# Mix products between two column groups of an attention product, and tiles turned by TensorE in an attention, channel-mix and expert kernel

## The chip, the cores and the metric

The kernel runs on one core of a Trainium2 chip. The metric is the device time of one execution in microseconds (us). Before the change the median of three runs is 1425.25 us (1423.19, 1425.25 and 1433.6).

## The reference, cut to what matters

```python
def reference(q, k, v, p, w_ch1, w_ch2, w_gate, w_local, w1, w2):
    # attention: B=8, H=8, S=576, D=64, 32 packed queries p per head
    packed = softmax(p @ k.T / 8) @ v            # 32 x 64 per head
    x = softmax(q @ packed.T / 8) @ packed       # (8, 576, 512) once the heads are side by side
    # mix: two-dimensional Fourier transform, layer norm, channel MLP 512 -> 2048 -> 512
    u = x + real(fft(fft(x, axis=1), axis=2))
    x = u + relu(layernorm(u) @ w_ch1) @ w_ch2
    # experts: 8 of them, 512 -> 1024 -> 512, one per token
    logits, gate = x @ w_gate, sigmoid(x @ w_local)
    for each token s of a batch in turn:
        e = argmax(logits[s]) if s == 0 or gate[s] < 0.5 else e of token s - 1
        out[s] = softmax(logits[s])[e] * (relu(x[s] @ w1[e]) @ w2[e])
    return out
```

## The kernel before

**Numbers and tiles.** Every fp32 operand is held as a high and a low fp16 half, and a product is three matmuls (`PASS`: high by high, high by low, low by high). Tokens go in tiles of 128; a block of the main part is one batch's 512 tokens, and the 64 tokens that each batch has over are gathered in two half blocks, "R0" and "R1".

**Main part.** The loop runs over the blocks 0, 1, 2, R0, 3, 4, 5, 6, R1, 7. For each, `Mix.mm1` (L1129, PSUM tiles hp) and `Mix.mm2` (L1149, PSUM tiles acc) make the channel MLP, 512 columns a matmul. After each few matmuls `tick` advances generators in the background, each at its own rate: the attention of the next block (with its Fourier transform), `after_mix` of the block before, and, from block 1 on, the cast of the expert weights into halves (`ew`). What a generator issues at a tick stands at that place of the queue of its engine, so the yields of a generator set where its work lies between the mix matmuls. A scheduler puts the instructions of each engine into their final order before the kernel runs, close to that order.

**The attention's cosine product.** Late in the attention, `products(cs, hf, tiles)` (L574 for the first two row tiles, L571 for the third) multiplies the even and odd parts eh with a table of cosines cst into the PSUM tile bp. For cs = 0 there are two column groups, hf = 0 and 1, with one bp tile each. `halves` (L579 on ScalarE, L580 on VectorE) copies a finished bp tile to SBUF. The bp tiles, the logits' lp, and others come from `att`, a PSUM pool with two buffers: a tile that is asked for waits until the last reader of the tile two before it is done.

**After the mix.** `after_mix` takes the tiles of a finished block one by one. VectorE makes a scale for each row, ScalarE (L1180) and VectorE (L1181) write the two halves into xh (tag hl, three buffers, which the gathered xg tiles use too), SyncE's queue (SP) transposes xh with a DMA into xt (L1188, one buffer) and writes xh to the DRAM table XS (L1189). A few yields later `logits` multiplies xt with the gate's weights (L1166, L1168, 18 and 9 columns, PSUM tile lp), and VectorE reduces lp to lsum (L1170). For block 7, whose mix ends the main part, `after_mix` runs at the start of the expert phase, beside the first expert blocks.

**Expert phase.** A line of 34 blocks of 128 tokens with one expert and 3 shared blocks with two experts of 64 tokens each. `load_x` gathers the tokens (L1491, GpSimd) and transposes them with a DMA on SP (L1495). `e1` (L1536, PSUM ehp, 96 matmuls of 128 columns) and `e2` (L1597, PSUM eo, 24 matmuls of 512 columns) are the two layers, and `e1` of a block runs ahead of `e2` of the block before. Expert weights come from DRAM by `weights` (L1517, queue SP) in quarters of 512 KB, into three slots. A shared block's first layer, `e1_two` (L1559), leaves its halves hh with tokens on partitions; `turned` (L1577) turns them by 16 matmuls against an identity into an `att` tile, from which ScalarE (L1582) and VectorE (L1580) copy them to hx. Before, `turned` is handed to `e2` of the block in front and runs between its matmuls. A second generator, `r1`, holds the rest of `after_mix` and the second routing, and must be done before the sixth block from the start.

Of the kernel before, what the change touches and what calls it, by code (L numbers as in the profile page):

```python
# [192 lines left out]
def _build(tc, nc, ctx, A, stop):  # L193
# [150 lines left out]
    def attention(b):  # L344
# [79 lines left out]
        for hf in range(2):  # L424
# [9 lines left out]
            n = 0  # L434
# [147 lines left out]

        for hf in range(2):
            products(0, hf, (0, 1))
        yield
        for hf in range(2):
            products(0, hf, (2,))
# [569 lines left out]
                        nc.vector.tensor_tensor(ut, ut, self.acc[j], op=ALU.add)  # L1157
            tick(0.25)

    def after_mix(tiles):  # L1160
        xt = None

        def logits(col):
            lp = att(f"lp{col}")
            for c in range(4):
                nc.tensor.matmul(lp[:, :18], xt[:, c], wgh[:, c].rearrange("p y e -> p (y e)"), start=c == 0, stop=False,  # L1166
                                 skip_group_check=True)
                nc.tensor.matmul(lp[:, :9], xt[:, 4 + c], wgh[:, c, 0], start=False, stop=c == 3, skip_group_check=True)  # L1168
            lsum = wp.tile([128, 9], F32, tag="lsum", name=f"lsum{col}", bufs=2)
            nc.vector.tensor_reduce(lsum, lp[:, :18].rearrange("p (y e) -> p e y", y=2), axis=AX.X, op=ALU.add)  # L1170
            nc.vector.tensor_scalar(LG[:, col], lsum, RSC[:, col:col + 1], 2.0 ** -20, ALU.mult, ALU.mult)

        for j, (ut, col) in enumerate(tiles):
            sc = wp.tile([128, 2], F32, tag="rsc", name=f"rsc{col}", bufs=2)
            nc.vector.tensor_reduce(sc[:, 0:1], ut, axis=AX.X, op=ALU.max, apply_absolute_value=True)
            nc.vector.tensor_scalar(RSC[:, col:col + 1], sc[:, 0:1], 1e-30, 0.25, ALU.max, ALU.mult)
            nc.vector.reciprocal(sc[:, 1:2], RSC[:, col:col + 1])
            yield
            hl = wp.tile([128, 1024], F16, tag="hl", name=f"xh{col}", bufs=3)
            nc.scalar.activation(hl[:, :512], ut, AF.Copy, scale=sc[:, 1:2])  # L1180
            nc.vector.scalar_tensor_tensor(hl[:, 512:], ut, sc[:, 1:2], hl[:, :512], ALU.mult, ALU.subtract)  # L1181
            yield
            if j:
                yield
                logits(tiles[j - 1][1])
                yield
            xt = wp.tile([128, 8, 128], F16, tag="xt", name=f"xt{col}", bufs=1)
            nc.sync.dma_start_transpose(out=xt, in_=hl)  # L1188
            nc.sync.dma_start(XS[128 * col:128 * col + 128], hl)  # L1189
            yield  # L1190
        for _ in range(4):
            yield
        logits(tiles[-1][1])
        yield
# [288 lines left out]

    w1b, w2b = [], []
    xg, xt, regs, hb = {}, {}, {}, {}

    def load_x(b):
        mp = M["p"]
# [33 lines left out]
    def load_w2(b, k0=0, k1=4):  # L1522
        weights(b, w2b, WS2, k0, k1)

    def e1(b, todo=()):

        ht = M["q"].tile([128, 2, 2, 512], F16, tag="hx", name=f"hx{b}", bufs=3)
        r = place_of(b)
        for fg in range(2):
            hp = (psM, psO)[fg].tile([128, 512], F32, tag="ho"[fg], name=f"ehp{b}_{fg}")  # L1530
            for f in range(4):
                n = 0
                cols = slice(128 * f, 128 * f + 128)
                for c in range(4):
                    for (x, y) in PASS:
                        nc.tensor.matmul(hp[:, cols], w1b[r][:, 2 * c + fg, x, cols], xt[b][:, 4 * y + c],  # L1536
                                         start=n == 0, stop=n == 11, skip_group_check=True)
                        n += 1
                if f % 2 == 0:
                    for fn, t in todo:  # L1540
                        fn(t, 2 * fg + f // 2, 2 * fg + f // 2 + 1)
                if f < 3:
                    tick()
            nc.scalar.activation(ht[:, fg, 0], hp, AF.Relu)  # L1544
# [1 line left out]
            tick()  # L1546
        hb[b] = ht

    def e1_two(b, todo=()):

        hh = M["q"].tile([128, 2, 2, 512], F16, tag="hx", name=f"hh{b}", bufs=3)
        for fg in range(2):
# [16 lines left out]
    def turned(b):  # L1569
        hh = hb[b]  # L1570
        ht = M["q"].tile([128, 2, 2, 512], F16, tag="hx", name=f"hx{b}", bufs=3)
        for fg in range(2):
            for x in range(2):
                tp = att(f"ht{b}_{fg}_{x}")
                for f in range(4):
                    cols = slice(128 * f, 128 * f + 128)
                    nc.tensor.matmul(tp[:, cols], hh[:, fg, x, cols], idh, start=f == 0, stop=True,  # L1577
                                     skip_group_check=True)
                if x:
                    nc.vector.tensor_copy(ht[:, fg, x], tp)  # L1580
                else:
                    nc.scalar.copy(ht[:, fg, x], tp)  # L1582
                yield
        hb[b] = ht

    def e2(b, todo=(), beside=None):
        h = hb.pop(b)
        op = psO.tile([128, 512], F32, tag="o", name=f"eo{b}")
        two = b >= FIRST
# [2 lines left out]
        for f in range(8):  # L1592
# [7 lines left out]
            if f % 2 == 0:  # L1600
                for fn, t in todo:
                    fn(t, f // 2, f // 2 + 1)
            if beside is not None and 2 <= f:
                next(beside, None)
            tick()
        ys = wp.tile([128, 512], F32, tag="U", name=f"ys{b}", bufs=8)
        nc.scalar.activation(ys, op, AF.Copy, scale=scl[:, b:b + 1])  # L1607
# [46 lines left out]
        prev = mix  # L1654
    for f in range(16 - LEAD, 16):
        prev.mm2(f)
    last = after_mix(prev.tiles)
    drain(r0)
    wctx.close()
    M["q"] = ctx.enter_context(tc.tile_pool(name="mq", bufs=1, side="right"))  # L1660
# [33 lines left out]

    def open_one(i):
        b = line[i]
        (e1_two if b >= FIRST else e1)(b, todo("e1", i))

    open_one(0)
    for i, b in enumerate(line):  # L1700
        if i + RB == NEARLY:
            drain(r1)
        if i + AHEAD < len(line):
            load_x(line[i + AHEAD])
        beside = None
        if i + 1 < len(line):
            open_one(i + 1)
            if line[i + 1] >= FIRST:
                beside = turned(line[i + 1])
        if i == len(line) - 1:  # L1710
            left = nc.values_load(used[0:1, 2:3], min_val=0, max_val=NFULL + NHALF)  # L1711
        e2(b, todo("e2", i), beside)
        if i == len(line) - 4:
            tc.keep_in_program_order(nc.gpsimd.drain())  # L1714

    def alone(b):
        load_x(b)
        for t in turns(b):
# [5 lines left out]
                pass  # L1724
        else:
            e1(b)
        e2(b)

    def rare(b):
# [29 lines left out]
```

## Time and profile before

| | |
|---|---|
| median of three runs | 1425.25 us |
| profiled execution | 1422.04 us |
| its span | 1420.0 us |
| mean granted TensorE clock | 0.987 |
| PE busy | 1370.0 us, 96% of the span |
| PE weight load busy | 791.2 us |
| DVE / ACT / POOL busy | 696.6 / 516.1 / 379.2 us |
| DMA moved | 257.67 MB |

PE is TensorE, DVE VectorE, ACT ScalarE, POOL GpSimd, SP the queue of SyncE. Matmuls are pipelined: a row's duration runs from its first start to its last end, and the rate of a run of matmuls is read from one row's start to the next one's. A bracket behind a row is idle time of the engine before it, and what ended it. The clock is the granted share of full speed: 1.00 is the upper of its two levels (2.4 GHz), 0.50 the lower (1.2 GHz).

### The profile page before, as it was taken

The numbers are of one execution on the slowest core, as the hardware profiler recorded it, in microseconds if no ns is written. First come the engines' busy times: TensorE is split into PE (matmuls) and PEld (weight loads), VectorE is DVE, ScalarE is ACT, GpSimd is POOL, SyncE is SP. The second block draws the span as 40 slices with busy tenths as digits, with TensorE's granted clock in tenths as the row PEclk, the third lists the DMA queues.
The fourth block names the chain that finished last, engine by engine and source line by source line (L and its number), as shares of the span: only waits on it lengthen the run. The fifth ranks groups of instructions, "written<-read, shape, count | busy, mean of one in ns | idle before, by whom it ended". The sixth has DMA issues, their size and how long they took to land. (4 is left out here: it accounts for less than half of the span.)

```text
span 1420.0 us, 27686 instructions
## 1 busy us (share of the span) xinstructions
PE 1370.0 (96%) x10812; PEld 791.2 (56%) x10812; DVE 696.6 (49%) x1415; ACT 516.1 (36%) x950; POOL 379.2 (27%) x386
## 2 busy tenths in 40 slices
PE   7799999999999999999999999999999999999998
PEld 5553445444564544444544456446577777776654
DVE  5799856657534655665665755433561111111111
ACT  2443365554355545445445444211211111111111
POOL 1002243443422434343344252000121211212101
PEclk8999999999999999999999999999999999999999
DMA  7465384784567558558557457244969668858881
GB/s 262 160 211 197 91 237 124 172 237 121 137 171 209 156 150 214 142 147 219 139 153 197 121 148 166 58 194 129 261 145 318 180 190 250 264 149 239 280 275 44
DMA packets 223864, 257.67 MB, mean 181 GB/s; under 512 B 155887, under 2 KB 167279, under 8 KB 221040
## 3 DMA queue, kind: packets, MB, share of 16 engines
q1 hardware_dynamic: 217648, 236.44, 58.9%
q0 software_dynamic: 6080, 19.40, 4.2%
q8 instruction: 87, 1.43, 0.4%
q14 instruction: 49, 0.40, 0.1%
HBM read 267.52 MB, written 52.95 MB: 226 GB/s over the span
## 5 line engine op out<-in xcount | busy, mean ns | idle before, releaser
L1149 PE MATMUL acc<-w,ht 128*128 128x512 f16 x1728 | 409.5, 379 | 0.0
L1129 PE MATMUL hp<-ut,w 128*128 128x512 f16 x1536 | 365.9, 380 | 3.8 <-DMA ut<-unh 2.5
L1129 PEld LDWEIGHTS <-w 128*128 128x128 f16 x1920 | 183.1, 98 | 183.0 <-issue 11.4
L1149 PEld LDWEIGHTS <-ht 128*128 128x128 f16 x1728 | 165.7, 98 | 188.6 <-issue 8.6
L337 POOL TENSOR_TENSOR halfs<-stage,halfs 128x512 f16<-128x512 f32 x128 | 151.2, 1187 | 294.6 <-ACT halfs L336 279.0
L1597 PE MATMUL eo<-w2b,hx 128*128 128x512 f16 (+1 forms) x984 | 210.7, 382 | 0.0
L1536 PE MATMUL ehp<-xgt,w1b 128*128 128x128 f16 x3360 | 202.0, 220 | 3.2 <-DMA w1b<-WS 3.2
L1536 PEld LDWEIGHTS <-w1b 128*128 128x128 f16 x3360 | 194.0, 99 | 16.5 <-DMA w1b<-WS 3.7
L1545 DVE SCALAR_TENSOR_TENSOR hx<-ehp,hx 128x512 f16<-128x512 f32 x70 | 48.3, 691 | 294.5 <-ACT hx L1544 294.5
L1137 DVE SCALAR_TENSOR_TENSOR ht<-hp,ht 128x512 f16<-128x512 f32 (+1 forms) x160 | 101.2, 633 | 154.9 <-ACT ht L1136 153.9
L1136 ACT ACTIVATE ht<-hp 128x512 f16<-128x512 f32 (+1 forms) x160 | 88.1, 550 | 233.5 <-PE hp L1129 228.6
L1597 PEld LDWEIGHTS <-hx 128*128 128x128 f16 (+1 forms) x984 | 87.5, 100 | 99.9 <-issue 8.6
L1608 POOL DMA_INDIRECT out<-ys,sidx x38 | 41.0, 1079 | 291.3 <-ACT ys L1607 266.4
L1544 ACT ACTIVATE hx<-ehp 128x512 f16<-128x512 f32 x70 | 41.8, 597 | 163.7 <-PE ehp L1536 163.5
L1607 ACT ACTIVATE ys<-eo,scl 128x512 f32<-128x512 f32 x38 | 26.1, 687 | 170.5 <-PE eo L1597 170.5
L336 ACT CAST halfs<-stage 128x512 f16<-128x512 f32 x128 | 77.6, 615 | 9.3 <-DMA WS<-halfs 5.5
L1491 POOL DMA_INDIRECT xg<-XS,gidx x38 | 40.5, 1066 | 141.1 <-DVE sidx L1458 51.5
L335 ACT ACTIVATE stage<-stage 128x512 f32<-128x512 f32 x128 | 77.7, 623 | 0.2
L362 POOL TENSOR_TENSOR qh<-q,qh 128x1420 f16<-128x1420 f32 x12 | 34.6, 2882 | 51.6 <-ACT qh L361 51.5
L1129 PE MATMUL hp<-utr,w 128*128 128x256 f16 x384 | 47.1, 272 | 0.0
L574 PE MATMUL bp<-cst,eh 128*128 128x289 f16 (+1 forms) x168 | 26.2, 291 | 12.9 <-DVE lsum L1170 9.6
L539 POOL TENSOR_TENSOR eo<-ee 128x256 f32<-128x256 f32 (+1 forms) x21 | 17.0, 811 | 77.2 <-DVE ee L523 74.0
(408 smaller groups left out, 1388.2 us busy)
## 6 DMA issues: line engine op xcount, KB each, us to landing
w1b<-WS SPq DMA_DIRECT2D x156, 512.0 KB
w2b<-WS SPq DMA_DIRECT2D x156, 512.0 KB
stage<-in_w SPq DMA_DIRECT2D x64, 512.0 KB
WS<-halfs SPq DMA_DIRECT2D x128, 256.0 KB
q<-in_qd SPq DMA_DIRECT2D x16, 710.0 KB
v<-in_vd SPq DMA_DIRECT2D x16, 640.0 KB
k<-in_kd SPq DMA_DIRECT2D x16, 576.0 KB
XS<-xh SPq DMA_DIRECT2D x36, 256.0 KB
```

The source lines that it names most:

```text
L335: nc.scalar.activation(st[:, a], st[:, a], AF.Copy, scale=64.0 if k < 4 else 256.0)
L336: nc.scalar.copy(so[:, 0], st[:, a])
L337: nc.gpsimd.tensor_tensor(so[:, 1], st[:, a], so[:, 0], op=ALU.subtract)
L1129: nc.tensor.matmul(hp[:, :ntok], w12[:, f, 0, x, 128 * c:128 * c + 128], ut[:, 4 * y + c, :ntok], start=n == 0, stop=n == 11)
L1136: pace[1] = nc.scalar.activation(ht[:, 0, :ntok], hp[:, :ntok], AF.Relu).ins
L1137: pace[0] = nc.vector.scalar_tensor_tensor(ht[:, 1, :ntok], hp[:, :ntok], 0.0, ht[:, 0, :ntok], ALU.max, ALU.subtract).ins
L1149: nc.tensor.matmul(self.acc[j], ht[:, x, 128 * j:128 * j + 128], w12[:, f, 1, y], start=f == 0 and n == 0, stop=f == 15 and n == 2)
L1536: nc.tensor.matmul(hp[:, cols], w1b[r][:, 2 * c + fg, x, cols], xt[b][:, 4 * y + c], start=n == 0, stop=n == 11, skip_group_check=True)
L1544: nc.scalar.activation(ht[:, fg, 0], hp, AF.Relu)
L1545: nc.vector.scalar_tensor_tensor(ht[:, fg, 1], hp, 0.0, ht[:, fg, 0], ALU.max, ALU.subtract)
L1597: nc.tensor.matmul(op[rows], h[:, f // 4, x, c0 + rows.start:c0 + rows.stop], w2b[r + a][:, f, y], start=n == 0, stop=n == 23, skip_group_ ...
L1608: nc.gpsimd.indirect_dma_start(out=A["out"], out_offset=bass.IndirectOffsetOnAxis(ap=sidx[:, b:b + 1], axis=0), in_=ys, in_offset=None, bo ...
```

## The change

Line numbers after the change are those of the new file: `products` keeps L574 and L571, the mix matmuls are L1131 and L1151, the turns L1167, the logits L1179 and L1181, the XS write L1206, `load_x`'s transpose L1513, the weight loads L1535, `e1` L1554, `e2` L1610.

1. In the attention of blocks 2 to 7 two yields stand between the column groups hf = 0 and hf = 1 of the first cosine product.
2. `turn_half` is new: four matmuls against the identity into one `att` tile and one copy out. `after_mix` has a form that turns xh with it, in two halves of four matmuls, and is used for the four tiles of block 7 alone; their DMA transposes are gone, the copies are on ScalarE (first half) and VectorE (second half), and one closing yield is left of four.
3. `turned` of a shared block moves from beside `e2` of the block in front to beside `e1` of the block behind it, one half after every second group of twelve matmuls, and each is held behind the newest `e1` matmul.

```diff
         for hf in range(2):
             products(0, hf, (0, 1))
+            if hf == 0 and b >= 2:
+                yield from wait(2)
...
+    def turn_half(dst, src, nm, x):
+        tp = att(nm)
+        for c in range(4):
+            cols = slice(128 * c, 128 * c + 128)
+            nc.tensor.matmul(tp[:, cols], src[:, cols], idh, start=c == 0, stop=True, skip_group_check=True)
+        if x:
+            nc.vector.tensor_copy(dst, tp)
+        else:
+            nc.scalar.copy(dst, tp)
...
-            nc.sync.dma_start_transpose(out=xt, in_=hl)
+            if by_pe:
+                for x in range(2):
+                    turn_half(xt[:, 4 * x:4 * x + 4], hl[:, 512 * x:512 * x + 512], f"xtp{col}_{x}", x)
+            else:
+                nc.sync.dma_start_transpose(out=xt, in_=hl)
             nc.sync.dma_start(XS[128 * col:128 * col + 128], hl)
             yield
-        for _ in range(4):
+        for _ in range(1 if by_pe else 4):
             yield
...
+                if f % 2:
+                    next(beside, None)
...
-                tp = att(f"ht{b}_{fg}_{x}")
-                for f in range(4):
-                    cols = slice(128 * f, 128 * f + 128)
-                    nc.tensor.matmul(tp[:, cols], hh[:, fg, x, cols], idh, start=f == 0, stop=True,
-                                     skip_group_check=True)
...
+                with tc.issue_after(newest[0]) if newest[0] is not None else nullcontext():
+                    turn_half(ht[:, fg, x], hh[:, fg, x], f"ht{b}_{fg}_{x}", x)
...
-            if beside is not None and 2 <= f:
-                next(beside, None)
...
-    last = after_mix(prev.tiles)
+    last = after_mix(prev.tiles, True)
...
+        beside = turned(line[i - 1]) if i and line[i - 1] >= FIRST else iter(())
+        (e1_two if b >= FIRST else e1)(b, todo("e1", i), beside)
```

The queue of PE at block 5's cosine product, before (weight loads and repeats of a row are left out; bp_0 and bp_1 are the two column groups, hp and acc the mix):

```order
L1129 MATMUL hp_9_6070<-ut_5126,w_130 128x512
...
L574 MATMUL bp_0_0_6093<-cst,eh_0_5986 128x289
...
L574 MATMUL bp_0_0_6093<-cst,eh_1_6013 128x289
...
L574 MATMUL bp_1_0_6100<-cst,eh_0_5986 128x289
...
L574 MATMUL bp_1_0_6100<-cst,eh_1_6013 128x289
...
L1129 MATMUL hp_9_6070<-ut_5126,w_130 128x512
...
L571 MATMUL bp_0_0_6093<-cst,eh_2_6047 128x289
```

And after the change:

```order
L574 MATMUL bp_0_0_6093<-cst,eh_0_5986 128x289
...
L574 MATMUL bp_0_0_6093<-cst,eh_1_6013 128x289
...
L1131 MATMUL hp_9_6070<-ut_5142,w_130 128x512
...
L1151 MATMUL acc_5508<-w_130,ht_7_5951 128x512
...
L574 MATMUL bp_1_0_6119<-cst,eh_0_5986 128x289
...
L574 MATMUL bp_1_0_6119<-cst,eh_1_6013 128x289
...
L1151 MATMUL acc_5509<-w_130,ht_7_5951 128x512
...
L571 MATMUL bp_0_0_6093<-cst,eh_2_6047 128x289
```

Before, nothing stands between the two column groups, and six hp matmuls between the second group and the L571 matmuls. Now those six and three acc matmuls stand between the groups, and six further acc matmuls between the second group and L571.

The queue of SP at the start of the expert phase, before (xh and xt are block 7's tiles, w1b weights, xgt gathered tokens):

```order
L1517 DMA w1b_10097<-WS_128 128x2048
L1188 DMA_TRANSPOSE xt_10182<-xh_10166 128x8x128
L1189 DMA XS<-xh_10166 128x1024
...
L1188 DMA_TRANSPOSE xt_10257<-xh_10217 128x8x128
L1189 DMA XS<-xh_10217 128x1024
L1495 DMA_TRANSPOSE xgt_10282<-xg_10278 128x8x128
...
L1517 DMA w1b_9398<-WS_128 128x2048
L1188 DMA_TRANSPOSE xt_10357<-xh_10317 128x8x128
L1189 DMA XS<-xh_10317 128x1024
```

And after the change:

```order
L1535 DMA w1b_10097<-WS_128 128x2048
L1206 DMA XS<-xh_10166 128x1024
...
L1206 DMA XS<-xh_10228 128x1024
L1513 DMA_TRANSPOSE xgt_10304<-xg_10300 128x8x128
...
L1535 DMA w1b_9398<-WS_128 128x2048
L1206 DMA XS<-xh_10339 128x1024
```

The four transposes of block 7's tiles are gone from SP; the rest of its queue keeps its order.

The queue of PE in the first two expert blocks, before (lp are the logits):

```order
L1536 MATMUL ehp_0_10118<-xgt_10102,w1b_9398 128x128
...
L1536 MATMUL ehp_1_10203<-xgt_10102,w1b_9398 128x128
...
L1536 MATMUL ehp_0_10285<-xgt_10108,w1b_9399 128x128
...
L1536 MATMUL ehp_1_10378<-xgt_10108,w1b_9399 128x128
...
L1166 MATMUL lp_10232<-wgh,xt_10182 128x18
L1168 MATMUL lp_10232<-wgh,xt_10182 128x9
```

And in the first of them after the change (xtp are the turns):

```order
L1554 MATMUL ehp_0_10118<-xgt_10102,w1b_9398 128x128
...
L1167 MATMUL xtp_0_10183<-c_97,xh_10166 128x128
...
L1554 MATMUL ehp_1_10214<-xgt_10102,w1b_9398 128x128
...
L1167 MATMUL xtp_1_10189<-c_97,xh_10166 128x128
...
L1554 MATMUL ehp_1_10214<-xgt_10102,w1b_9398 128x128
...
L1179 MATMUL lp_10243<-wgh,xt_10182 128x18
```

The first turn stands behind 44 matmuls of the block's `e1`, the second 8 later, and the first tile's logits 20 later; before, the logits stood behind 188 `e1` matmuls. The third tile's turn stands behind 177.

## Rows read from the trace of the kernel before

**Rows 1.** Waits of PE, whole span: us in total, times, longest us.

```profile
PE bp L574 <- DVE lsum L1170: 9.6, 5, 2.7
...
PE ehp L1536 <- DMA w1b<-WS: 3.2, 3, 1.5
...
PE hp L1129 <- DMA ut<-unh: 2.5, 1, 2.5
```

**Rows 2.** Timeline of PE: start us, us, operation, times, idle before; attention of blocks 5 and 6.

```profile
587.16 0.91 PE L574 MATMUL bp<-cst,eh 128*128 128x289 f16 x6
590.75 1.61 PE L574 MATMUL bp<-cst,eh 128*128 128x289 f16 x6 [2.69 <-DVE lsum L1170]
...
697.72 0.90 PE L574 MATMUL bp<-cst,eh 128*128 128x289 f16 x6 [1.92 <-DVE lsum L1170]
```

**Rows 3.** Timeline of PE, end of the main part and start of the expert phase.

```profile
975.43 7.93 PE L1149 MATMUL acc<-w,ht 128*128 128x512 f16 x36
983.20 10.66 PE L1536 MATMUL ehp<-xgt,w1b 128*128 128x128 f16 x188
995.67 0.18 PE L1166 MATMUL lp<-wgh,xt 128*128 128x18 f16 x1 [1.81 <-DMA xt<-xh]
...
996.11 6.17 PE L1597 MATMUL eo<-w2b,hx 128*128 128x512 f16 x20
...
1032.05 5.62 PE L1536 MATMUL ehp<-xgt,w1b 128*128 128x128 f16 x51 [1.53 <-DMA w1b<-WS]
```

**Rows 4.** Windows: us, busy us (count) by engine, PE's clock, DMA share, GB/s.

```profile
590.70:594.10 3.40, 3.35 (x11) 1.62 (x11) 0.23 (x1) 0.20 (x1) 1.15 (x1) 0.50 0.66 203
996.90:1000.30 3.40, 3.40 (x10) 1.18 (x8) 1.44 (x2) 0.72 (x2) 0.00 (x0) 0.50 1.25 220
1032.10:1037.80 5.70, 5.70 (x53) 5.65 (x54) 3.01 (x5) 0.60 (x1) 2.23 (x1) 0.50 0.77 239
1016.00:1020.00 4.00, 3.40 (x59) 2.84 (x58) 2.81 (x8) 0.31 (x2) 0.30 (x1) 1.00 1.17 254
...
1024.00:1028.00 4.00, 4.00 (x22) 1.88 (x20) 3.96 (x27) 0.00 (x0) 1.03 (x1) 1.00 0.99 401
```

**Rows 5.** Groups by line, the shared blocks' turns: busy us, mean ns, idle before.

```profile
L1577 PE MATMUL ht<-c,hh 128*128 128x128 f16 x48 | 4.2, 219 | 2.0 <-ACT hx L1582 1.2 <-DVE hh L1566 0.8
...
L1582 ACT CAST hx<-ht 128x512 f16<-128x512 f32 x6 | 3.5, 584 | 3.1 <-PE ht L1577 3.1
```

**Rows 6.** Timelines of PE, ACT and DVE: a bp tile's way to SBUF.

```profile
237.18 0.29 PE L571 MATMUL bp<-cst,eh 99*128 99x288 f16 x1
...
237.51 0.41 ACT L579 ACTIVATE big<-bp 128x288 f16<-128x288 f32 x1 [1.63 <-PE bp L571]
237.95 0.46 DVE L580 SCALAR_TENSOR_TENSOR big<-bp,big 128x288 f16<-128x288 f32 x1 [1.02 <-ACT big L579]
```

**Rows 7.** Timelines of DVE and ACT: halves of block 7's first, third and fourth tile.

```profile
986.10 0.75 DVE L1181 SCALAR_TENSOR_TENSOR xh<-ul,rsc,xh 128x512 f16<-128x512 f32 x1 [0.47 <-ACT xh L1180]
...
997.64 0.72 ACT L1180 ACTIVATE xh<-ul,rsc 128x512 f16<-128x512 f32 x1 [0.74 <-DVE hx L1545]
1001.76 0.72 ACT L1180 ACTIVATE xh<-uu,rsc 128x512 f16<-128x512 f32 x1 [3.40 <-DMA XS<-xh]
```

**Rows 8.** Timeline of SP's issues in the same stretch.

```profile
986.88 3.84 SPq L1188 DMA_TRANSPOSE xt<-xh  x1
990.77 0.58 SPq L1189 DMA_DIRECT2D XS<-xh  x1
...
997.35 0.57 SPq L1189 DMA_DIRECT2D XS<-xh  x1
...
1007.51 1.62 SPq L1188 DMA_TRANSPOSE xt<-xh  x1
...
1014.38 3.08 SPq L1517 DMA_DIRECT2D w1b<-WS  x4
```

**Rows 9.** DMA from 955 to 967 us, three xgt transposes: packets, MB, share of 16 engines.

```profile
q1 hardware_dynamic: 3168, 0.79, 45.3%
```

More of the change, by code (lines that the diff above doesn't have):

```diff
@@ L1158, in mm2, with after_mix @@
             tick(0.25)
-    def after_mix(tiles):
+    def turn_half(dst, src, nm, x):
[7 more added lines that the diff above has]
+            nc.scalar.copy(dst, tp)
+    def after_mix(tiles, by_pe=False):
         xt = None
@@ L1485, in _build @@
     xg, xt, regs, hb = {}, {}, {}, {}
+    newest = [None]
     def load_x(b):
@@ L1523, in load_w2, with e1 @@
         weights(b, w2b, WS2, k0, k1)
-    def e1(b, todo=()):
+    def e1(b, todo=(), beside=iter(())):
         ht = M["q"].tile([128, 2, 2, 512], F16, tag="hx", name=f"hx{b}", bufs=3)
@@ L1535, in e1 @@
                     for (x, y) in PASS:
-                        nc.tensor.matmul(hp[:, cols], w1b[r][:, 2 * c + fg, x, cols], xt[b][:, 4 * y + c],
-                                         start=n == 0, stop=n == 11, skip_group_check=True)
+                        newest[0] = nc.tensor.matmul(hp[:, cols], w1b[r][:, 2 * c + fg, x, cols], xt[b][:, 4 * y + c],
+                                                     start=n == 0, stop=n == 11, skip_group_check=True).ins
                         n += 1
@@ L1547, in e1, with e1_two @@
         hb[b] = ht
-    def e1_two(b, todo=()):
+    def e1_two(b, todo=(), beside=None):
         hh = M["q"].tile([128, 2, 2, 512], F16, tag="hx", name=f"hh{b}", bufs=3)
@@ L1573, in turned, with e2 @@
             for x in range(2):
-                tp = att(f"ht{b}_{fg}_{x}")
-                for f in range(4):
-                    cols = slice(128 * f, 128 * f + 128)
-                    nc.tensor.matmul(tp[:, cols], hh[:, fg, x, cols], idh, start=f == 0, stop=True,
-                                     skip_group_check=True)
[L1579 to L1582, printed above, removed]
+                with tc.issue_after(newest[0]) if newest[0] is not None else nullcontext():
+                    turn_half(ht[:, fg, x], hh[:, fg, x], f"ht{b}_{fg}_{x}", x)
                 yield
         hb[b] = ht
-    def e2(b, todo=(), beside=None):
+    def e2(b, todo=()):
         h = hb.pop(b)
@@ L1696, in open_one @@
         b = line[i]
-        (e1_two if b >= FIRST else e1)(b, todo("e1", i))
+        beside = turned(line[i - 1]) if i and line[i - 1] >= FIRST else iter(())
+        (e1_two if b >= FIRST else e1)(b, todo("e1", i), beside)
+        for _ in beside:
+            pass
     open_one(0)
@@ L1704, in _build @@
             load_x(line[i + AHEAD])
-        beside = None
         if i + 1 < len(line):
             open_one(i + 1)
-            if line[i + 1] >= FIRST:
-                beside = turned(line[i + 1])
         if i == len(line) - 1:
             left = nc.values_load(used[0:1, 2:3], min_val=0, max_val=NFULL + NHALF)
-        e2(b, todo("e2", i), beside)
+        e2(b, todo("e2", i))
         if i == len(line) - 4:
             tc.keep_in_program_order(nc.gpsimd.drain())
+    newest[0] = None
     def alone(b):
@@ L1726, in alone @@
             e1(b)
+            newest[0] = None
         e2(b)
```

## The prediction

> **What bounds the kernel now.** I read the waits of PE first, since the table has PE busy nearly throughout: time can be won where PE stands idle and where its clock is low. The waits view [rows 1] gives two entries that the change touches: five times 9.6 us in all of the attention's cosine product waiting for VectorE's lsum, and 3.2 us of the first expert layer waiting for weights. Then the timeline of PE at the lsum waits [rows 2]: for block 5, column group hf = 0 starts at 587.16 and takes 0.91 us, group hf = 1 follows 2.69 us late; for block 6 the wait is 1.92, the next longest. What is left of the 9.6 is 5.0 us for three more. The reason lies in the two buffers of the PSUM pool: group hf = 1 asks for the one that lsum still has to read. Third, the timeline where the main part passes into the expert phase [rows 3]: the logits of block 7's first tile wait 1.81 us for a transposed tile, and the weights come last at 1032.05. Fourth, the windows behind those waits [rows 4]: after the 2.69 us wait the granted clock is 0.50 (the lower level) for 3.4 us, after the 1.81 us wait for 3.4, after the weights' wait for 5.7. In the other four lsum stretches no such fall is seen. Last, the shared blocks' turns [rows 5]: 2.0 us of waiting for the copies out of PSUM.
>
> **Part 1, two yields in the cosine product.** Nothing is added; nine mix matmuls move. Their rate is 0.216 us (36 of them from 975.43 to 983.20 [rows 3]), so they cover 1.94 us. VectorE's order up to lsum is as before, so lsum comes when it did. The four waits up to 1.92 vanish; of block 5's 2.69, 0.75 stays. That is 9.6 - 0.75 = 8.8 us. With 0.75 instead of 2.69 I also take the fall of the clock behind it as gone: half of 3.4 us, 1.7.
> What is late next? For b >= 2 the product with cs = 1 takes the buffer that hf = 0 leaves, so its matmuls must find that tile copied. The copy's way is a last matmul, ScalarE, VectorE: from 237.18 to 237.95 + 0.46 in one row of each [rows 6], 1.23 us. After the change six mix matmuls (1.30 us) and one L571 matmul (about 0.12) stand there in PE's queue, 1.42 us, so 0.2 is spare: I take 0.5 us over six blocks, bounds 0 and 1.5 (a quarter of a microsecond each). The attention as a whole ends two yields later, about the nine matmuls' 1.94 us; what reads its result is the next block's first hp, which in the whole span waits for that transpose only once [rows 1], so I cost this at nothing; without that slack it would be up to 1.94 us in each of six blocks, which the range does not take in.
>
> **Part 2, tiles turned by TensorE.** Removed is the wait of 1.81 us [rows 3] and the fall of the clock behind it: 20 eo matmuls took 6.17 us, and half of 3.4 us [rows 4] is 1.7. Added are 8 turns of four 128-column matmuls. One such costs 0.056 us (188 from 983.20 in about 10.5 us [rows 3]); 32 make 1.8 us, all on PE's path.
> New waits: the first turn stands behind 44 e1 matmuls, at 983.20 + 44 x 0.056 = 985.7, and xh's high half is done about 986.10, its low half at 986.85 [rows 7]: 0.4 and then 0.1 us, behind which all of e1 is queued. The logits now stand some 20 matmuls (1.1 us) behind the second turn, whose copy takes about 0.58 us [rows 5] plus hand-offs: 0.1 to 0.2 us for two of four tiles. Third and fourth tile share xh buffers with the first and second, whose XS write must have landed. Before, that write was issued behind the transpose, at 990.77 [rows 8], and had landed by 997.64; the second, issued at 997.35, landed at 1001.76, in 4.4 us [rows 7, 8]. So 4.4 to 6.9 us; issued now right behind xh, at 986.9, it lands between 991.3 and 993.8, and the third tile's high half is ready by 994.5. The turn stands behind 177 e1 matmuls, 16 turns and 16 logits: about 995.4. It just holds. I take 2.0 us for all of these waits, with 0.5 and 6 as bounds.
> The transposes' DMA time goes too. The weights that PE waits for at 1028 to 1032 are issued at 1014.38, behind the fourth transpose at 1007.51 [rows 8]. Three like transposes of gathered tokens filled 45.3% of 16 engines for 12 us [rows 9], 1.8 us each; four make 7.2, against weights that come 3.2 us late in all. So that wait goes, 3.2 us, and with it the low clock of 5.7 us [rows 4], 2.85. The XS writes stay as they are.
> The Trainium skill, "Advanced Engine Details and Errata", section "X-Bar Transpose (TRN2)", says that on this chip transposing DMAs are as fast as regular ones. By the row of the three transposes they are not, here: at the 401 GB/s of the window from 1024 [rows 4] a 262 KB tile would take 0.65 us, four 2.6. By that rule 0.6 us of the weights' wait, and perhaps the low clock, would stay, and the sum would be some 3.4 us smaller; I go by the row of those transposes.
>
> **Part 3, the shared blocks' turns.** 48 matmuls before, 48 after. Beside e2 each turn found its PSUM buffer still being copied (584 ns a copy) or its halves unfinished: 2.0 us [rows 5]. Beside e1 a turn comes only after 24 matmuls, 1.3 us, so the copy is covered; I take the 2.0 us as won, bounds 0 and 2.2. What hides behind it, e2 of the shared block, comes a whole e1 later than its first turn, so it does not wait.
>
> **Sum.** -8.8 - 1.7 + 0.5 (part 1), -1.81 - 1.7 + 1.8 + 2.0 - 3.2 - 2.85 (part 2), -2.0 (part 3) = -17.75. From the profiled execution, 1422.04 us, that gives 1404.3. The median of the runs is 3.2 us above the profiled one, so 1407.5 in its terms.
>
> **Rivals.**
> A, the weights stay late. DMA was 99% busy from 1024 to 1028 [rows 4]; if what the transposes leave is filled by weights issued earlier for other blocks, 3.2 + 2.85 = 6.05 us stay: 1413.5. For it: the queue keeps its order. Against it: the bytes in front of those weights become fewer. Chance 0.14.
> B, third and fourth tile wait for the XS writes. If these land as slowly as the first transpose did (986.88 to 995.67, 8.8 us [rows 3, 8]), xh's high half is ready at 996.4, 1.0 us late; the fourth about 0.6; a fall of the clock of 1.7 behind each makes 5.0 in all: 1412.5. Against it: two writes landed in 4.4 and at most 6.9 us. Chance 0.13.
> C, the wait for lsum turns into a wait of the cs = 1 product behind ScalarE, which casts expert weights in that part. A cast in front of the copy (as long as the 0.58 us one of [rows 5]) and one on VectorE behind it would make some 1.1 us, in six blocks 6.6: 1414.1. For it: the spare time is 0.2 us. Against it: in the rows shown ScalarE takes the tile up 0.04 us after the matmul's end [rows 6]. Chance 0.11.
> D, slower. PE's clock falls at each of the 12 new places in the first expert blocks where it depends on another engine (8 turns, 4 logits). At 1.7 us a fall that is 20.4, and the waits come to 6 instead of 2: 1422.04 - 17.75 + 20.4 + 4 = 1428.7, or 1431.9 beside the median; if each fall lasts 5.7 us, 1446. It decides against me once more than ten falls happen. For it: three of the waits read above had one. Against it: from 1016 to 1020 PE idles 0.60 of 4 us and holds clock 1.00 [rows 4], and the four shorter lsum waits left it alone. Chance 0.04.
> E, nothing is won, since other waits take up all of it in the attention and in the experts alike: 1425. Chance 0.02.
>
> **How the numbers follow.** Forecast 0.56, its own range 1404 to 1411 (2.0 us of new waits down to 0.5 and 0.5 to 0 gives 1405.5; a little more clock gives 1404; up 3.5 for larger waits gives 1411). A measurement of this kernel tells about 1%, 14 us, from no change, so faster begins below 1411. A, B and C lie just above that bound; two of them together give 1419. Range 1400 to 1419. Faster 0.57 (forecast and a small part of C), same 0.40 (A, B, most of C, E and the smaller form of D), slower 0.03 (the longer D).
>
> **What would show it.** Right: no wait of L574 for lsum but one below 1 us at block 5, no clock of 0.50 near 590, logits at the start of the expert phase without waits over 0.3 us, no wait of e1 for w1b near 1028, no wait of the turns in the last 100 us. Wrong: waits of the turns (now L1167) for xh or of xh for XS, of cs = 1 products for bt's copies, or a row for w1b as before. If the waits are gone and the time is not, the mean clock must have fallen below 0.987, or the windows of the first expert blocks show it.

## The result, and the profile after

The changed kernel takes 1412.88 us in the median of 6 runs (1410.57 to 1416.96), the one before 1425.74 beside it; the ratio is 0.9905, with a 95% interval of 0.988 to 0.993. That is 13.5 us (10 to 17) less; 17.75 were forecast. Two of the runs used below are in a slower state (1763.75 us of the kernel before, 3292.88 of "later cs = 1, four closing yields") and stand in no median and no ratio here. The profiled execution after takes 1412.99 us, its span is 1411.0, 9.0 less than before.

The waits of PE after the change, in the view of [rows 1] (total, times, longest, in us):

```profile
PE ep L1285 <- DVE e L1275: 1.8, 2, 1.4
...
PE tabf L1440 <- DVE stage L1451: 1.6, 1, 1.6
PE pps L438 <- DVE vhl L428: 1.5, 2, 1.3
PE xtp L1167 <- ACT xh L1193: 1.5, 2, 1.2
PE bp L574 <- DVE big L580: 1.4, 1, 1.4
...
PE bp L574 <- DVE lsum L1183: 0.7, 1, 0.7
```

The 9.6 us of lsum waits are 0.7, all of it at block 5, as forecast. The waits for w1b are gone, and those of the turns for hx and hh; the 1.81 us wait for xt is gone too. In their place stand four others: the second routing's tabf, the third turn of block 7's tiles (xtp for xh), vhl, and the copy of a bp tile (big); and ep, also of the second routing, has grown from 1.0 to 1.8.

Windows after the change, in the columns of [rows 4]; first two stretches that lie ahead of everything that the change touches, then what stands now where before had its three low-clock stretches (the last behind tabf's wait):

```profile
132.90:136.40 3.50, 3.49 (x10) 1.39 (x11) 3.50 (x7) 1.12 (x1) 0.35 (x1) 0.51 0.58 246
180.70:184.20 3.50, 3.39 (x11) 1.07 (x15) 1.11 (x2) 0.00 (x0) 0.00 (x0) 0.51 0.00 0
594.20:597.60 3.40, 3.37 (x20) 1.85 (x20) 1.48 (x4) 2.52 (x6) 2.36 (x3) 1.00 0.69 212
995.00:998.40 3.40, 3.33 (x29) 1.74 (x28) 1.79 (x6) 1.81 (x3) 0.52 (x1) 1.00 0.45 132
1021.10:1026.80 5.70, 5.57 (x52) 3.90 (x53) 5.70 (x10) 0.60 (x1) 1.35 (x1) 1.00 0.93 295
```

The same two early stretches before the change:

```profile
131.60:135.10 3.50, 3.50 (x18) 1.68 (x19) 3.50 (x7) 1.13 (x1) 0.35 (x1) 1.00 0.55 232
178.30:181.80 3.50, 3.50 (x22) 1.31 (x23) 1.76 (x9) 0.03 (x1) 0.00 (x0) 1.00 0.00 0
```

In the third number from the end of a row, the clock, lies a trap. The first two stretches hold the same instructions in both kernels, behind the same two waits of about 2.5 us, and yet PE ran at the lower level in the one execution and at full clock in the other: 1.7 us lost twice. So the difference of the two spans, 9.0 us, hides some 3 us of gain, and whether a wait is followed by a fall is not fixed by the program.

To compare stages without this, the table gives the time between the starts of the same matmuls in every profiled execution: from the start to the 205th hp matmul (A, ahead of the change), on to the first e1 matmul (B, the mix with the attention), to the 1033rd e1 matmul (C, block 7's tiles and the second routing), to the 2881st (D, untouched), and to the last second-layer matmul of the line (E, the shared blocks). Each is worked out from two starts in the timeline of PE.

| profiled execution | A | B | C | D | E |
|---|---|---|---|---|---|
| before | 181.6 | 801.6 | 122.3 | 203.5 | 104.9 |
| after | 185.7 | 794.4 | 120.9 | 204.6 | 99.4 |
| after, again | 181.0 | 793.9 | 121.0 | 206.2 | 99.4 |
| part 1 alone | 185.2 | 795.3 | 119.4 | 206.2 | 104.9 |
| part 2 alone | 181.7 | 799.9 | 120.6 | 205.9 | 104.9 |
| part 3 alone | 185.7 | 801.4 | 119.1 | 205.7 | 99.4 |
| second layer held | 181.8 | 801.4 | 120.8 | 205.6 | 102.2 |
| one yield | 183.3 | 806.5 | 119.7 | 203.5 | 99.5 |
| later cs = 1 | 182.7 | 790.7 | 120.1 | 203.5 | 99.4 |
| four closing yields | 181.5 | 795.0 | 120.2 | 203.5 | 99.4 |
| transposes kept | 184.0 | 796.8 | 122.8 | 203.5 | 99.4 |
| later cs = 1, four closing yields | 187.2 | 791.1 | 122.3 | 204.9 | 99.4 |
| later cs = 1, without part 2 | 184.6 | 791.0 | 123.0 | 205.6 | 99.4 |

A and D hold the same work throughout and still vary by 6 and by 2.7 us: that is the noise of one profile. B varies by 1.7 us in the four kernels without part 1 (mean 801.1), E repeats to 0.1 us. Between the first two profiles B fell by 7.2, E by 5.5, C by 1.4 us; the forecast had 10.0, 2.0 and 5.8.

### The profile page after: what moved, and what is told of

It is laid out like the page before. It is cut to its first block, busy times and chain, and to the rows that moved or that the text cites. A ratio compares the mean times of both kernels' runs of the same rounds, so it can differ in the third digit from the quotient of the medians.

```text
span 1411.0 us, 27771 instructions
## 1 busy us (share of the span) xinstructions
PE 1366.9 (97%) x10844; PEld 791.0 (56%) x10844; DVE 700.6 (50%) x1419; ACT 517.4 (37%) x954; POOL 377.0 (27%) x386
## 5 line engine op out<-in xcount | busy, mean ns | idle before, releaser
L1151 PE MATMUL acc<-w,ht 128*128 128x512 f16 x1728 | 412.1, 379 | 0.1
L1131 PE MATMUL hp<-ut,w 128*128 128x512 f16 x1536 | 367.4, 381 | 3.1 <-DMA ut<-unh 2.4
L1131 PEld LDWEIGHTS <-w 128*128 128x128 f16 x1920 | 183.5, 98 | 184.5 <-issue 13.8
L1151 PEld LDWEIGHTS <-ht 128*128 128x128 f16 x1728 | 165.8, 98 | 187.9 <-issue 10.1
L1610 PE MATMUL eo<-w2b,hx 128*128 128x512 f16 (+1 forms) x984 | 207.5, 379 | 0.0
L1554 PE MATMUL ehp<-xgt,w1b 128*128 128x128 f16 x3360 | 202.2, 219 | 0.5 <-PE ehp L1554 0.4
L1554 PEld LDWEIGHTS <-w1b 128*128 128x128 f16 x3360 | 192.7, 98 | 15.4 <-issue 3.4
L1610 PEld LDWEIGHTS <-hx 128*128 128x128 f16 (+1 forms) x984 | 87.2, 100 | 95.0 <-issue 3.3
L1131 PE MATMUL hp<-utr,w 128*128 128x256 f16 x384 | 47.1, 272 | 0.6 <-DVE ht L1139 0.6
L722 POOL TENSOR_TENSOR unh<-un,unh 128x512 f16<-128x512 f32 x28 | 31.8, 1159 | 17.9 <-ACT unh L721 15.4
```

Of the source, the lines that this page charges most:

```text
L1131: nc.tensor.matmul(hp[:, :ntok], w12[:, f, 0, x, 128 * c:128 * c + 128], ut[:, 4 * y + c, :ntok], start=n == 0, stop=n == 11)
L1151: nc.tensor.matmul(self.acc[j], ht[:, x, 128 * j:128 * j + 128], w12[:, f, 1, y], start=f == 0 and n == 0, stop=f == 15 and n == 2)
L1554: newest[0] = nc.tensor.matmul(hp[:, cols], w1b[r][:, 2 * c + fg, x, cols], xt[b][:, 4 * y + c], start=n == 0, stop=n == 11, skip_group_ch ...
L1610: nc.tensor.matmul(op[rows], h[:, f // 4, x, c0 + rows.start:c0 + rows.stop], w2b[r + a][:, f, y], start=n == 0, stop=n == 23, skip_group_ ...
```

## The experiments

### Each part alone

Three kernels, each the one before with one part of the change: the two yields,

```diff
             products(0, hf, (0, 1))
+            if hf == 0 and b >= 2:
+                yield from wait(2)
```

`turn_half` and its use for block 7's tiles, with one closing yield,

```diff
-    last = after_mix(prev.tiles)
+    last = after_mix(prev.tiles, True)
```

and the move of `turned` with all that belongs to it:

```diff
+        beside = turned(line[i - 1]) if i and line[i - 1] >= FIRST else iter(())
+        (e1_two if b >= FIRST else e1)(b, todo("e1", i), beside)
```

> The kernel before with the two yields in the cosine product alone. From the trace of the changed kernel (first theory): the lsum waits fall from 9.6 to about 0.7 us, a wait of the cs = 1 product for VectorE's copy of about 1.4 us appears in block 3's attention and one of about 1.3 us for vhl in block 6's, and the stretch from block 1's mix to the first expert matmul is about 7.3 us shorter; time -6 to -8 us. By the prediction's sum: -10.0 us, no new wait above 0.3. Rival (new waits eat the gain): -3 us or less.

> The kernel before with block 7's tiles turned by TensorE alone. First theory, from the trace of the changed kernel: the waits for xt (1.81) and for w1b (3.2) go, waits of the second routing's matmuls for VectorE and of the third turn for xh (together about 4.5 us) take their place, no stretch at clock 0.50 from 980 to 1060, and the stretch from the first expert matmul to the 1032nd is 1 to 2 us shorter; time -1 to -3. By the prediction's sum: -5.8 us. Rival: the routing's waits alone decide and it is not faster, 0 to +2 us.

> The kernel before with the shared blocks' turns beside the following first layer alone. First theory: from the 2880th first-layer matmul to the end 5 to 5.5 us shorter, of which 2.0 are the turns' waits, about 2.4 the 144 second-layer matmuls of half width that now run in one stretch for each block (18.5 to 16.1 us busy), and the rest the turns and first layers beside them; time -4 to -6 us. By the prediction's sum: -2.0 us. Rival (the gain in the last stretch belongs to the parts before it): -2 us or less.

Measured against before (1424.65 us in the median of 30 runs): part 1 alone 1418.47, ratio 0.9956 (0.9935 to 0.9977), 6.3 us less; part 2 alone 1424.08, ratio 0.9998 (0.998 to 1.0015), nothing; part 3 alone 1420.22, ratio 0.9966 (0.9946 to 0.9986), 4.8 us less. The three add up to 11.4 us, within the interval of the whole. The interval of part 2 alone, -2.9 to +2.1 us, leaves out the forecast 5.8.

For part 1, B fell by 6.3 us and the two side waits are there. Its waits of PE:

```profile
PE lp L1168 <- DMA xt<-xh: 2.8, 3, 1.8
...
PE pps L438 <- DVE vhl L428: 2.3, 3, 1.2
...
PE tabf L1425 <- DVE stage L1436: 1.6, 1, 1.6
...
PE bp L574 <- DVE big L580: 1.4, 1, 1.4
...
PE bp L574 <- DVE lsum L1172: 0.7, 1, 0.7
```

No row for w1b stands among them (its one wait of e1, 1.6 us, lies at 1298.77, far behind), though this kernel has all four transposes and, from the first e1 matmul up to the shared blocks, the very order of instructions of before on every compute engine. PE waits 1.6 us for VectorE's stage instead, a wait that before lay hidden behind the one for the weights. In part 3 alone, again with the order of before in that stretch, the wait for w1b is 1.4 us, in the kernel of the next experiment 2.5, in the last one below, which has part 2 left out, 2.7, before 3.2. Part 3 alone, and the last one:

```profile
PE ehp L1552 <- DMA w1b<-WS: 1.4, 1, 1.4
```

```profile
PE ehp L1556 <- DMA w1b<-WS: 2.7, 2, 1.6
```

So the size of that wait is a matter of the execution: 3.2, 0, 1.4, 2.5 and 2.7 us for the same instructions, in the mean 2.0, with a fall of the clock there in three of the five. The falls elsewhere behave alike. Part 3 alone, behind the lsum wait of 2.69 us and behind the xt wait of 1.70:

```profile
594.60:598.00 3.40, 3.38 (x11) 1.55 (x11) 0.23 (x1) 0.16 (x1) 1.15 (x1) 0.53 0.68 210
999.50:1002.90 3.40, 3.40 (x26) 1.78 (x27) 1.81 (x4) 1.32 (x2) 0.00 (x0) 1.00 1.48 329
```

and part 2 alone, behind the same lsum wait of 2.69 us:

```profile
590.70:594.10 3.40, 3.36 (x19) 1.84 (x19) 0.72 (x2) 1.31 (x5) 1.16 (x1) 1.00 0.67 206
```

The one falls where the other doesn't. C in the five executions that have before's order there (before, part 1, part 3, second layer held, later cs = 1 without part 2) is 122.3, 119.4, 119.1, 120.8 and 123.0, in the mean 120.9; in the seven whose tiles TensorE turns, without the transposes, it is 119.7 to 122.3, in the mean 120.7. In none of the seven does e1 wait for w1b at that place. The wait that part 2 was to remove is gone, and still nothing is won: all seven have a wait of 1.4 to 1.9 us for VectorE's stage, one of 0.9 to 1.6 us of the third turn, and 32 more matmuls. The 1.4 us by which C fell in the first pair of profiles lie within the spread of the five.

### Why the last stretch gained more than its waits

The kernel before, with the first second-layer matmul of a shared block held (`newest` is kept in `e1` as in the change):

```diff
+                    with tc.issue_after(newest[0]) if two and n == 0 and newest[0] is not None else nullcontext():
                         nc.tensor.matmul(op[rows], h[:, f // 4, x, c0 + rows.start:c0 + rows.stop], w2b[r + a][:, f, y],
                                          start=n == 0, stop=n == 23, skip_group_check=True)
```

> The kernel before, in which only the second layer of a shared block is held behind the newest first-layer matmul, so that its 48 half-width matmuls stand in one stretch; the turns stay where they were. If cutting up that stretch costs time: these 144 matmuls take about 16 us instead of 18.5, the turns' 2.0 us of waits stay, time -1.5 to -3.5 us. If the gain of the last stretch comes from the turns' waits alone: no change beyond 0.5 us, 18.5 us as before.

Measured: 1423.47 us, ratio 0.9985 (0.9962 to 1.0007): by the times alone not settled. By the profile it is: E is 102.2 us, 2.7 less than before, the turns' 2.0 us of waits stay, and the half-width matmuls of the second layer take as long as after the change. The groups by line and shape in the last stretch, before:

```profile
L1597 PE MATMUL eo<-w2b,hx 128*64 128x512 f16 x144 | 18.5, 383 | 0.0
```

and in this kernel:

```profile
L1600 PE MATMUL eo<-w2b,hx 128*64 128x512 f16 x144 | 16.1, 380 | 0.0
```

The timeline of PE before shows what was slow, the second layer of the second shared block:

```profile
1357.32 2.36 PE L1597 MATMUL eo<-w2b,hx 128*64 128x512 f16 x11
1359.61 0.51 PE L1536 MATMUL ehp<-xgt,w1b 128*128 128x128 f16 x6
1360.04 3.01 PE L1597 MATMUL eo<-w2b,hx 128*64 128x512 f16 x18
...
1368.74 3.64 PE L1597 MATMUL eo<-w2b,hx 128*64 128x512 f16 x31
```

and after the change:

```profile
1360.54 5.37 PE L1610 MATMUL eo<-w2b,hx 128*64 128x512 f16 x48
1365.84 0.51 PE L1554 MATMUL ehp<-xgt,w1b 128*128 128x128 f16 x6
```

In one stretch 48 of them take 5.30 us, 0.11 each, half of the 0.216 of a full one: the two half-width matmuls of a pair run side by side. The Trainium skill says so in "TensorE: Matmul & The Clock Gate", section "Part 3: Packing small matmuls — row/col tiling": small matmuls at different places of the array run at the same time; the rows agree.

The rows of before need care: the timeline joins neighbours of one line and shows the shape of the first. Groups by shape for the first of them, from 1357.30 to 1359.55:

```profile
L1597 PE MATMUL eo<-w2b,hx 128*128 128x512 f16 x6 | 1.5, 381 | 0.0
L1597 PE MATMUL eo<-w2b,hx 128*64 128x512 f16 x5 | 1.0, 398 | 0.0
```

Of the 11 only five are half-width; the other six are another block's at full width, between them. In the same way 12 of the 18 are half-width. So the 48 stood in pieces of 3, 2, 10, 2 and 31, two of them odd, where one matmul runs without its partner. The last stretch has six such single ones, at 0.216 instead of 0.108 us: 0.65 us. The greater part is a price of changing the width: between a matmul of full width and one of half width, either way, the next start comes 0.09 to 0.12 us later than behind one of its own kind (above, six e1 matmuls from 1359.61 at 0.056 us end their turn at 1359.95, and the half-width ones start at 1360.04). Counted over the whole trace of the last stretch, E has 50 such changes before, and 32 in this kernel as after the change; 18 fewer are some 1.8 us.

So of the 5.5 us in E, 2.7 come from the second layer that stays together (1.8 from the changes of width, 0.65 from the partners), 2.0 from the waits, and 0.8 are left. Of these some 0.65 can belong to the waits too, by an estimate from the rows: a wait is counted from the end of the last matmul, 0.22 us behind its start, while without a wait the next one starts 0.056 us behind it, which makes 0.16 more for each of the four waits.

### How much cover, and where the attention falls

The changed kernel with one yield,

```diff
-                yield from wait(2)
+                yield from wait(1)
```

and the changed kernel with the cs = 1 product one yield later:

```diff
         yield
+        if b >= 2:
+            yield
         products(1, 0, (0, 1, 2))
```

> The changed kernel with one yield instead of two between the column groups. If the cover is what counts: about 1 us of mix matmuls instead of 1.94 stands there, lsum waits of about 0.8, 0.6, 1.7, 0.9 and 0.6 us come back (4.6 in all), and the stretch from block 1's mix to the first expert matmul is 2 to 4 us longer than after the change. If the side waits that the later attention brings (1.41 for the copy in block 3's attention, about 1.5 for vhl in block 6's) count for as much: they go with the second yield and the stretch is as long as after the change, within 1 us.

> The changed kernel with one more yield ahead of the product with cs = 1, in blocks 2 to 7. If that product waits because the copy of the first group is held up in ScalarE's queue by a cast (theory): the wait of 1.41 us falls to 0.5 or less and the stretch of block 2's mix is about 1.4 us shorter; the stretch up to the first expert matmul 1 to 2 us shorter than after the change. If the wait follows the product (a rival: whatever is placed there waits for VectorE): a wait of more than 1 us stays, and no gain.

One yield: 1417.91 us, ratio 0.9969 (0.995 to 0.9988). B is 806.5 us, 12.1 more than after the change, far more than either theory had; falls of the clock at 345 and 639 us that the change's profile does not have are in it. Its waits of PE:

```profile
PE s L383 <- issue: 6.1, 4, 1.9
PE bp L574 <- DVE lsum L1183: 3.0, 5, 1.4
PE bp L574 <- DVE big L580: 2.3, 1, 2.3
```

and the window behind the 2.3:

```profile
345.40:348.90 3.50, 3.50 (x12) 1.56 (x11) 0.46 (x1) 0.41 (x1) 0.00 (x0) 0.51 0.65 211
```

The lsum waits came back with 3.0 us, less than expected; but the one yield that is gone moved the whole rest of the attention, and the first scores s of the next attention now wait three times 1.9 us. The trace names no releaser for them; the nearest event at the first, at 274.33, is the end of VectorE's last read of the P tile at 273.82 + 0.41, a reader in the same PSUM pool; that this is what they wait for is not shown. So a yield has two effects, the cover at its place and a shift of everything behind it, and the second can be the greater.

Later cs = 1: 1404.98 us, ratio 0.9876 (0.9852 to 0.99), the fastest of all: some 17.6 us below before. The wait of 1.41 us is gone, as the theory had it, and B is 790.7, 3.7 us less, where 1 to 2 were expected: the waits for vhl, 1.5 us after the change, do not appear either. Where that wait comes from can be read in the timelines of PE, ACT and DVE after the change:

```profile
342.55 0.81 PE L1131 MATMUL hp<-ut,w 128*128 128x512 f16 x3
344.77 0.90 PE L574 MATMUL bp<-cst,eh 128*128 128x288 f16 x6 [1.41 <-DVE big L580]
...
343.29 0.62 ACT L336 CAST halfs<-stage 128x512 f16<-128x512 f32 x1 [1.84 <-DMA WS<-halfs]
343.81 0.71 ACT L579 ACTIVATE big<-bp 128x289 f16<-128x289 f32 x2
...
344.25 0.83 DVE L580 SCALAR_TENSOR_TENSOR big<-bp,big 128x289 f16<-128x289 f32 x2 [2.60 <-ACT big L579]
```

The copy of the bp tile (L579) is ready to go near 342, but stands in ScalarE's queue behind a cast of expert weights, and this cast waits 1.84 us until a DMA write has freed its buffer. One more yield puts the cs = 1 product behind that.

### What part 2 does

The changed kernel with four closing yields,

```diff
-        for _ in range(1 if by_pe else 4):
+        for _ in range(4):
```

and the changed kernel with the DMA transposes besides the turns:

```diff
             if by_pe:
                 for x in range(2):
                     turn_half(xt[:, 4 * x:4 * x + 4], hl[:, 512 * x:512 * x + 512], f"xtp{col}_{x}", x)
+                spare = M["q"].tile([128, 8, 128], F16, tag="spare", name=f"spare{col}", bufs=1)
+                nc.sync.dma_start_transpose(out=spare, in_=hl)
```

> The changed kernel with four closing yields behind block 7's last tile, as before the change, instead of one. If the second routing's matmuls wait for VectorE since they stand three yields earlier (theory): the waits of 1.39 and 1.64 us fall to about 0.6 and 0.3, and the stretch from the first expert matmul to the 1032nd is about 2 us shorter; time -1 to -2 us against the changed kernel. Rival (VectorE's chain sets the pace of the routing, and PE only meets it elsewhere): the waits keep their sum within 0.7 us, no change.

> The changed kernel, in which block 7's tiles are turned by TensorE and, besides, transposed by the four DMAs into a tile that nobody reads (extra work that leaves the result as it is). By the prediction's step, that the DMA time of these transposes makes the weights late: the waits of the first layer for w1b come back with 1.5 to 3.5 us, time +2 to +6 us against the changed kernel. If the transposes are not what made the weights late (kernel before with the two yields alone has them and shows no such wait): 0 to 0.5 us of waits for w1b, time within 1.5 us of the changed kernel.

Four closing yields: 1407.73 us, ratio 0.9893 (0.9874 to 0.9912), C 120.2 us instead of 120.9. The wait of ep fell to 0.60, that of tabf stayed at 1.66, so the theory is half right at best; and the kernel with both edits below shows 1.45 for ep with the same four yields, while later cs = 1, with one closing yield, shows 0.60. The yields are not the cause. What sets this wait is left open.

Transposes kept: 1414.29 us, ratio 0.9927 (0.99 to 0.9954). There is no wait for w1b, though the four transposes are back on the queue. This does not decide the prediction's step, since the reader moved as well. The weights of the fifth block and its first e1 matmuls, in this kernel (timelines of SP and PE; its first e1 matmul starts at 980.81):

```profile
1010.88 3.43 SPq L1537 DMA_DIRECT2D w1b<-WS  x4
...
1033.21 0.83 PE L1556 MATMUL ehp<-xgt,w1b 128*128 128x128 f16 x12
```

and after the change (first e1 matmul at 980.06):

```profile
1005.15 2.66 SPq L1535 DMA_DIRECT2D w1b<-WS  x4
...
1031.15 1.11 PE L1554 MATMUL ehp<-xgt,w1b 128*128 128x128 f16 x17
```

Counted from the first e1 matmul, the weights are issued at 30.1 us here, 25.1 after the change and 31.2 before; PE comes to the fifth block at 52.4, 51.1 and 44.7, since the turns and, moved up, matmuls of the second routing (tabf) now stand in front of it with their waits. Before, the last weights let PE go on at 48.9: by that, weights issued about as late as before are in time for a PE that comes at 51 or 52.

What comes is a longer wait of the third turn. The kernel with the transposes kept, timelines of SP and ACT:

```profile
988.50 0.57 SPq L1208 DMA_DIRECT2D XS<-xh  x1
...
995.74 0.72 ACT L1193 ACTIVATE xh<-ul,rsc 128x512 f16<-128x512 f32 x1 [4.21 <-DMA XS<-xh]
```

and the changed kernel, timelines of SP, ACT and PE:

```profile
983.74 0.33 SPq L1206 DMA_DIRECT2D XS<-xh  x1
...
992.38 0.72 ACT L1193 ACTIVATE xh<-ul,rsc 128x512 f16<-128x512 f32 x1 [1.60 <-DMA XS<-xh]
...
993.15 0.40 PE L1167 MATMUL xtp<-c,xh 128*128 128x128 f16 x4 [1.16 <-ACT xh L1193]
...
1007.20 0.17 PE L1285 MATMUL ep<-c,e 4*128 4x4 f16 x1 [1.39 <-DVE e L1275]
...
1021.16 0.60 PE L1440 MATMUL tabf<-stage,owf 128*128 128x238 bf16 x4 [1.64 <-DVE stage L1451]
```

The first XS write is issued at 983.74 and lets go of its buffer at 992.38: 8.6 us. With the transposes kept it is issued behind the first of them, some 4 us later beside xh, and lands in 7.2, and the third turn waits 3.0 us instead of 1.2, with a fall of the clock behind it.

### The changed kernel once more, and two versions

The changed kernel as it is; with the two edits "later cs = 1" and "four closing yields" together; and with "later cs = 1" but without part 2:

```diff
-    last = after_mix(prev.tiles, True)
+    last = after_mix(prev.tiles)
```

> The changed kernel itself once more, beside the next two on the same chip. Against before 0.988 to 0.993 as measured. In its profile the waits of the code's own places return (0.74 for lsum, 1.4 for the copy in block 3's attention, about 1.2 for xh, 1.6 for stage); whether the clock falls near 133 and 181 us, ahead of anything that the change touches, and whether it falls near 997, is open by both theories: if falls belong to chance, at least one of them differs from the first profile.

> The changed kernel with both earlier edits: one more yield ahead of the cs = 1 product, and four closing yields. If their gains are apart (theory): about 3.6 us from the first (stretch of the mix blocks) and 1 us from the second (the wait for the scan's result 1.39 to 0.60), 4 to 5 us below the changed kernel, ratio to it 0.996 to 0.997. Rival: the first run's gain was a matter of one profile, less than 2 us.

> The kernel with the additional yield ahead of the cs = 1 product, but block 7's tiles transposed by DMA as before, with four closing yields: parts 1 and 3 of the change only. If part 2 gains nothing (theory, from its run alone): the same as the run before within 1.5 us. By the prediction's terms for part 2: 5.8 us slower than with it.

All three on one chip, before 1425.94: the changed kernel 1415.12, ratio 0.9932 (0.9908 to 0.9957); later cs = 1 with four closing yields 1409.99, ratio 0.989 (0.9862 to 0.9917); later cs = 1 without part 2 1411.83, ratio 0.9909 (0.9884 to 0.9934). B is 791 us in both, as in the first run of that edit, so its 3 us repeat. With and without part 2 differ by 1.8 us in the median, inside both intervals. Later cs = 1 with part 2 and one closing yield had 0.9876 on the same chip, 4.7 us below the 0.9909 without part 2, with intervals that overlap; so a few us of gain beside that edit are not ruled out, and that part 2 gains nothing rests on its run alone and on C. In the changed kernel's second profile the early stretches read:

```profile
129.50:133.00 3.50, 3.50 (x18) 1.68 (x19) 3.50 (x7) 1.14 (x1) 0.36 (x1) 1.00 0.60 253
176.10:179.60 3.50, 3.48 (x15) 1.05 (x15) 1.01 (x2) 0.00 (x0) 0.00 (x0) 0.52 0.00 0
```

The first fall of the first profile is not there, the second is: the same code, another execution.

## Why the prediction was right, and where it was not

The time lies in the range and the sign holds; the size was 18 for 13.5. The likeliest case did not come: by the prediction's own bound faster begins below 1411, and 1412.88 falls among "same", with chance 0.40, though the interval is clear of no change. That the sum is nearer than its terms are is luck: it gave part 1 3 to 4 us and part 2 some 6 us too much, and part 3 3.5 too little.

**Part 1**, forecast -10.0, measured 6 to 7 us less in B (from the mean of 801.1) and -6.3 in the times. Right: the cover of nine matmuls (9.6 us to 0.7, and 0.7 at block 5 as worked out), and the price of nothing for the later ut. Mis-sized is the term "I take 0.5 us over six blocks" for new waits: 1.4 us for the copy, still within its bound of 1.5, came by the mechanism of rival C, in one block instead of six, and 1.1 to 1.6 a wait for vhl near 560 us, early in block 5's attention (not block 6's, as the expectation says), were not foreseen, though the whole rest of that generator moved by two yields. The attention of block 4 had no lsum wait, and the mix beside it gained nothing. The clock's 1.7 us at 590 held in three of the four executions that still have the wait of 2.69 us, so it was a fair term, though not a sure one.

**Part 2**, forecast -5.8, measured 0 (ratio 0.9998). The step that failed is "So that wait goes, 3.2 us, and with it the low clock of 5.7 us", as a gain of 6.05 us. The wait does go, in all seven profiles without the transposes; but the sum took one profile's wait and one profile's fall for what the kernel always pays. The five executions with the same instructions there have 3.2, 0, 1.4, 2.5 and 2.7 us, in the mean 2.0, and a fall in three. It also missed that behind the weights' wait another one of 1.6 us (VectorE's stage) stood ready, which comes out when the first goes: part 1 alone shows it. And it gave the transposes' DMA time as the cause, which stays open: the weights are issued some 6 us earlier without the transposes, and PE comes to them some 6 us later. With the transposes put back, the weights are issued nearly as late as before and PE's coming later is enough; whether the earlier issue alone would be, no run shows. The new waits of the turns were sized 2.0; those for xh are 1.5, but by the mechanism of rival B: the XS write took 8.6 us, not 4.4 to 6.9 as the writes before the change, which stood elsewhere in the queue. The rule of the Trainium skill ("Advanced Engine Details and Errata", section "X-Bar Transpose (TRN2)") that on this chip transposing DMAs are as fast as regular ones, by which part of the weights' wait would have stayed, cannot be decided by that wait, for the same reason.

**Part 3**, forecast -2.0, measured -5.5 in E and -4.8 in the times. The waits were 2.0, as said. The step that failed is "48 matmuls before, 48 after": it priced the turns and not what their move does to the order of the second layer, which now stays together, for 2.7 us.

**The rivals.** A (weights late) did not come in the changed kernel. B and C came in part, each at one place, B in all seven profiles. D did not: of the new places where PE depends on another engine, none was followed by a fall in the two profiles of the changed kernel; the third turn was in the kernel with the transposes kept, behind 3.0 us.

## What to carry to other kernels

A wait, and even more a fall of the clock behind it, that one profile shows is one draw: before it is put into a sum, look for the same instructions in a second execution, and compare stages between the same matmuls rather than spans. When work is moved in a queue, price what is pulled apart or pushed together there, and what moves behind it, not the moved instructions alone. A wait that goes uncovers the next; ask what was ready just behind it. And a wait has two ends: before its going is put down to the one, see whether the reader comes later.

## What the hardware showed that was not expected

The clock's falls are not fixed by the program: behind the wait of 2.47 to 2.50 us near 130 us, which all 13 profiles have in the same code, it fell in 8 of them (for 3.4 us in three, 6.8 in five) and not in 5; behind the wait of 2.4 to 2.5 us near 180 it fell in 12 of 13. Behind the xt wait of 1.7 to 2.2 us it fell in four of five profiles.

Two half-width matmuls of a pair took the time of one (0.11 us each against 0.216) only where the pair stood together, and each change between full and half width put 0.09 to 0.12 us between two starts: in pieces between other matmuls 144 of them cost 18.5 us instead of 16.1, and 50 changes instead of 32 some 1.8 us of the stretch.

A write of 256 KB to DRAM that took 4.4 us to land at one place before the change took 8.6 after it, where it stands earlier in the same stage.
